# Fused top-k attention, mixture of experts and cosine layer: w_out converted beside the first experts, expert weights loaded ahead, six candidate segments

## The chip, the cores and the metric

One core of a Trainium2 chip runs the whole program. The metric is device time in microseconds of one launch, from host arrays in the chip's memory to the finished output there; lower is better. Engines are named as in the profile: PE is TensorE (matmul), DVE is VectorE, ACT is ScalarE, POOL is GpSimd, and SP is SyncE, which issues nearly all DMA transfers from one queue, in order.

## The reference, cut to what matters

Three layers follow one another: attention that keeps the 32 largest scores of each row, a mixture of experts with a skip test, and a dense layer pair with a cosine gate.

```python
# attention: q, k, v are [4, 8, 576, 64]
scores = scale * np.matmul(q, k.transpose(0, 1, 3, 2))
kth = np.partition(scores, -32, axis=-1)[..., -32:-31]
scores = np.where(scores >= kth, scores, -1e9)
attn = exp(scores - max); attn /= attn.sum(-1, keepdims=True) + 1e-9
x = (attn @ v) as [2304, 512]

# experts: w_gate [512, 8], w1 [8, 512, 1024], w2 [8, 1024, 512]
do_compute = x @ w_skip > 0
e_idx = argmax(x @ w_gate); gate_w = its softmax probability
y = gate_w * (relu(x @ w1[e_idx]) @ w2[e_idx])
x = x + y where do_compute, else x

# dense pair: w_in [512, 2048], w_out [2048, 512], stored as float64
h = x @ w_in
out = (h * cos(h)) @ w_out
```

[...]

## The kernel before, in words

**Two groups.** The 2304 tokens are two groups of 1152 (two batches each). For a group, `attend(n)` (line 559) runs 72 times: 8 heads times 9 tiles of 128 rows. One such call is named a step here; n counts from 0 to 71 for group 0 and from 72 to 143 for group 1. After its attention a group is stored, routed to experts (`route`, line 743), sent through the experts (`experts`, line 850) and through the dense pair (`cosine`, line 988). Group 0's experts and cosine layer run on PE between the attention steps of group 1; group 1's experts and cosine layer come last.

**A step.** PE computes scores into one of three PSUM slots `s` (L587). DVE takes the 8 largest of each of `NSEG` = 8 segments of 72 columns (L596), giving 64 candidates, and finds the 24th largest of these by three maxima (L606) and two replacements (L608). ACT computes the exponentials (L613) and, from the 24th candidate, which scores lie above it and how many (L617, L620). PE shifts those out of the way (L625), DVE finds the 8 largest of the rest (L633, 584 wide) and so the 32nd of the row, and masks (L636). ACT and POOL split the weights into two float16 parts (L639, L643, L644), SP transposes them by DMA (L647), and PE weighs the values (L654 to L663). A row is right as long as the count of scores at or above the 24th candidate is below 32; the flags from L1106 on test this for all rows, and a general path outside the plan repeats what fails.

**Converting the float64 weights.** `load_f64` (line 424 on) does one slice of 65,536 numbers (512 KB) at a time: SP loads it into one of two stage buffers `wbuf[0:2]` (L431), ACT takes the sign (L436), DVE shifts and merges the two integer halves (L437, L439), POOL and ACT build a range check (L441, L446), ACT scales (L443), POOL sets the sign (L448), ACT writes the high float16 part (L450) and POOL the low one (L451). The scratch is a ring of two for the bits and one buffer each for sign and magnitude; it lies in the gate slots 4 to 7 of the cosine layer (`r_gT`). There are 16 slices of w_in (`load_win`) and 16 of w_out (`load_wout`). In the kernel before, w_out has a buffer of its own, and its slices are declared after step 38 (`EARLY`) with priorities n + 4 + 2i, which is 42 to 72: among the steps of group 0.

**The expert weights.** Each expert has 4 tiles of w1 and 4 of w2, 512 KB each, 64 tiles in all per group, loaded by L862. Group 0's experts use them in float32 straight from the four buffers `wbuf[2:]` (the ring `r_wall`), so tile k waits until tile k - 4 has been read by PE. The first four may start when step 38 has passed its normalisation (`gate[n0 - 34]`). PE's work on them is at L911 (first matrix) and L942 (second).

**What sets the order.** All work is declared as units with an engine, a cost, what they read and write, and a priority (`Plan.add`). `Plan.run` (line 156) simulates the engines with these costs and issues the instructions in the order in which the simulation starts them; on each engine the ready unit with the smallest priority goes first, and that order is then fixed on the chip. Units with a priority from 900 up belong to group 0's experts and cosine layer; for ACT and DVE 1000 is taken off, and for POOL 2000, so there they go ahead of most attention steps, while on PE and SP they come after:

```python
SOONER = {"ACT": 1000.0, "DVE": 1000.0, "POOL": 2000.0}
if prio >= 900:
    prio -= self.SOONER.get(eng, 0.0)
```

SP issues no further load while the planned DMA backlog is over 3.5 us.

Of the kernel before, what the change touches and what calls it, by code (L numbers as in the profile page):

```python
# [10 lines left out]
F32 = mybir.dt.float32  # L11
F16 = mybir.dt.float16
# [191 lines left out]
def kernel(  # L204
# [14 lines left out]
    nc = tc.nc  # L219
    B, H, S, D = q.shape  # L220
    NT, DM = out.shape
# [9 lines left out]
    NFF = FF // P  # L231
# [4 lines left out]
    ESC = 1.0 / (math.sqrt(D) * SQ * SQ)  # L236
    HUGE = 2.0 ** 40 / ESC
    N = NG * H * NJ
    NSEG = 8
    EARLY = 38  # L240

    dram = ctx.enter_context(tc.tile_pool(name="dram", bufs=1, space=DRAM))
    x_d = [dram.tile([GT, DM], F32, name=f"x_d{g}") for g in range(NG)]
# [14 lines left out]
    def sb(name, shape, dt=F32):  # L258
        return pool.tile([P] + list(shape), dt, name=name)
# [4 lines left out]
    def as16(ap, *shape):  # L264

        t = ap.bitcast(F16)
        return view(t, *shape)
# [92 lines left out]


    win = Slot(sb("win16", [KD, 2, FF], F16), NFF)
    wout = Slot(sb("wout16", [NFF, 2, DM], F16), NFF)
    SPACE = 136064
    arena = Arena(sb("arena", [SPACE // 4]), SPACE)

    def ring(n, shape, dt=F32, parts=1):
        return Ring([arena.new(shape, dt, parts) for _ in range(n)])

    r_qkv = ring(2, [10, D])  # L370
    r_h16 = ring(2, [9, 2, D], F16, 2)
# [8 lines left out]
    for sl in r_v.slots:  # L380
        sl.ap = (view(sl.ap, 10, D + 1), view(sl.ap[:, 10 * (D + 1):], 10, D))
        nc.vector.memset(sl.ap[0][:, :, D:D + 1], SV)
    r_cand = ring(3, [8 * NSEG], F32, NSEG)
    r_m = ring(4, [48], F32, 5)
# [1 line left out]
    mj = ring(2, [P])  # L386
    xs = arena.new([NJ, DM], F32, 3)
    wbuf = [arena.new([1024]) for i in range(6)]
    free = [arena.at(4096 * i, [1024], F32) for i in range(9)]
    r_stage = [Ring(wbuf[:2]), Ring(wbuf[:2] + free[:5])]  # L390
    r_split = [Ring(wbuf[2:]), Ring(wbuf[2:] + free[5:])]
    r_wall = Ring(wbuf[2:])
    r_sq = ring(1, [DM], F16)
    x0 = xs.lo

    def after(base, n, shape, dt=F32, parts=1):

        size = 2048
        return Ring([arena.at(base + size * i, shape, dt, parts) for i in range(n)])

    r_x16 = [ring(2, [2, DM], F16, 2), after(36864, 2, [2, DM], F16, 2)]
    r_xT = [ring(2, [DM]), after(36864 + 4096, 2, [DM])]
    r_xg = [ring(3, [DM]), after(x0, 3, [DM])]
    r_gT = [ring(8, [DM], F32, 2), after(x0 + 6144, 4, [DM], F32, 2)]
    r_ob = [ring(2, [DM]), after(x0 + 14336, 2, [DM])]
# [9 lines left out]
    def dve(n):  # L415
        return (n + 64) / 960.0
# [57 lines left out]
                wmx[:, i:i + 1], pw.ap, axis=AX.X, op=OP.max), r=[pw], w=[mxs], prio=prio)  # L474

    def load_wout(i, prio):
        load_f64(wout, wout[i], wout.ap[:, i:i + 1, 0, :], wout.ap[:, i:i + 1, 1, :],
                 w_out.rearrange("(c p) d -> p c d", p=P)[:, i:i + 1, :], SO, NFF + i, prio)


    n0 = H * NJ
    heads = {}
    gate = Slot(parts=N)
# [75 lines left out]
    def attend(n):  # L559
# [33 lines left out]
        p, r, jk = r_p.new(), r_r.new(), r_jk.new()  # L593
        sw = S // NSEG
        for i in range(NSEG):
            add("DVE", dve(sw), lambda i=i: nc.vector.max(cand.ap[:, 8 * i:8 * i + 8], S_[:, sw * i:sw * i + sw]),  # L596
# [253 lines left out]
    def experts(g, prio):  # L850
        gs, gidx, sidx, rs = routed[g]
        wide = WIDE[g]
        scat = []
        xg, xT, hT, w = {}, {}, {}, {}

        def weight(e, s, i):
            if s == 0:
                src = w1[e].rearrange("(c p) f -> p c f", p=P)[:, :, i * 256:(i + 1) * 256]
            else:
                src = w2[e].rearrange("(c p) d -> p c d", p=P)[:, 2 * i:2 * i + 2, :]  # L860
            st = (r_wall if wide else r_stage[g]).new()
            add("SP", 0.5, lambda: nc.sync.dma_start(st.ap.rearrange("p (a b) -> p a b", a=src.shape[1]), src),  # L862
                r=[gate[n0 - 34]] if g == 0 else [], w=[st], prio=prio[0] - 5, lat=0.6, dma=1.5)
            if wide:
                w[e, s, i] = (st, view(st.ap, KD, 256) if s == 0 else view(st.ap, 2, DM))
                return
            sp = r_split[g].new()
            wv = as16(sp.ap, 2, 1024)
            sc = S2 if s else S1
            add("ACT", act(1024), lambda: nc.scalar.activation(wv[:, 0, :], st.ap, AF.Copy, scale=sc),  # L870
                r=[st], w=[sp], prio=prio[0] - 4)
            add("DVE", dve(1024), lambda: nc.vector.scalar_tensor_tensor(
                wv[:, 1, :], st.ap, sc, wv[:, 0, :], op0=OP.mult, op1=OP.subtract),
                r=[st], w=[sp], prio=prio[0] - 4)
            w[e, s, i] = (sp, as16(sp.ap, 2, KD, 256) if s == 0 else as16(sp.ap, 2, 2, DM))
# [112 lines left out]
    def cosine(g, prio):  # L988
# [45 lines left out]
        def output(i, fc, po):  # L1034
            gt, gv = gts[i, fc // 4]

            def mm():
                for n_, (sg, sw) in enumerate(((0, 0), (1, 0), (0, 1))):
                    nc.tensor.matmul(po.ap, gv[:, sg, fc % 4, :], wout.ap[:, fc, sw, :],  # L1039
                                     start=(fc == 0 and n_ == 0), stop=(fc == NFF - 1 and n_ == 2))  # L1040

            add("PE", 0.66, mm, r=[gt, wout[fc]], w=[po], prio=prio[0])
            prio[0] += 1
# [11 lines left out]
        for i in range(NJ + 1):  # L1055
            if i + 1 < NJ:
                turn(i + 1)
            po = ring_m[1 + 2 * g].new(True) if i else None
# [17 lines left out]
        load_win(i, 4.0 * i + 10.0)  # L1076
    for n in range(n0):
        attend(n)
        if n == EARLY:
            for i in range(NFF):  # L1080
                load_wout(i, n + 4.0 + 2.0 * i)
    recut(third_ps, [s2], half, "half", "right")
    store_x(0, n0 + 0.0)
    route(0, n0 - 10.0)
# [2 lines left out]
    recut(wide_ps, s_slots, quarter, "quarter", "left")  # L1087
    prio = [1000.0]
    experts(0, prio)
    cosine(0, prio)  # L1090
    store_x(1, 0.0)
    route(1, 0.0)
# [2 lines left out]
    prio = [4000.0]  # L1095
# [353 lines left out]
```

## Time and profile before

| | |
|---|---|
| median of 3 runs | 1208.11 us (1207.56 to 1214.32) |
| the profiled execution's own time | 1203.05 us |
| its span, first to last instruction | 1200.8 us |
| busy PE, DVE, ACT, POOL | 968.3, 878.0, 803.6, 576.5 us |
| share of the span | 81%, 73%, 67%, 48% |
| mean granted TensorE clock | 0.907 of full speed |
| DMA moved | 191.44 MB, mean 159 GB/s |

All rows further down are from that one execution. A busy time is the time in which the engine had an instruction in it; durations of single instructions overlap where an engine is pipelined. [...] "DMA" is the mean busy share of the 16 DMA engines. "L596" is line 596 of the kernel.

### The profile page before, as it was taken

What the parts mean: (1) busy time and instruction counts of PE and PEld (TensorE: products, weight loads), DVE (VectorE), ACT (ScalarE), POOL (GpSimd) and SP (SyncE); (2) the same over time, 40 slices, a digit from 0 to 9 for tenths busy, and PEclk for the clock granted to TensorE, in tenths of its full rate; (3) what the DMA queues carried; (4) which work ended last, traced back from release to release, by engine and by line L of the source; (5) the groups of instructions that cost most, each with busy time, mean ns of one, the idle gap of its engine ahead of it and who ended that gap; (6) DMA issues with size and microseconds to landing.
All of it is one profiled execution on the core that took longest, in us unless ns stands there. A gap on an engine that the chain in (4) does not pass through costs nothing. (4 is left out here: it accounts for less than half of the span.)

```text
span 1200.8 us, 27693 instructions
## 1 busy us (share of the span) xinstructions
PE 968.3 (81%) x9891; PEld 689.2 (57%) x9892; DVE 878.0 (73%) x3187; ACT 803.6 (67%) x1657; POOL 576.5 (48%) x591
## 2 busy tenths in 40 slices
PE   2656666665667788889868999998998999999996
PEld 1334444333445566666637766776775756777773
DVE  6999999998897876767787888996577874322221
ACT  5888898888776555656668777875466657543441
POOL 5989999888553434444443534342123321222121
PEclk9999996555657699999978999999999999999999
DMA  8767868778669599999997465449479972210100
GB/s 190 162 155 173 158 150 184 191 165 174 136 144 198 108 264 228 248 274 274 269 212 132 87 98 129 103 125 265 79 174 313 333 224 73 61 37 19 36 10 22
DMA packets 343124, 191.44 MB, mean 159 GB/s; under 512 B 260546, under 2 KB 313794, under 8 KB 342976
## 3 DMA queue, kind: packets, MB, share of 16 engines
q1 hardware_dynamic: 340416, 183.30, 65.7%
q0 software_dynamic: 2560, 6.28, 1.7%
q8 instruction: 79, 1.29, 0.5%
q14 instruction: 69, 0.57, 0.2%
HBM read 107.50 MB, written 18.35 MB: 105 GB/s over the span
## 5 line engine op out<-in xcount | busy, mean ns | idle before, releaser
L1009 PEld LDWEIGHTS <-win 128*128 128x128 f16 x3456 | 216.5, 99 | 49.8 <-issue 1.7
L596 DVE MAX8 arena<-s 128x8 f32<-128x72 f32 x1152 | 197.0, 224 | 26.7 <-PE s L587 26.3
L1031 POOL TENSOR_TENSOR arena<-arena 128x512 f16<-128x512 f32 x72 | 84.8, 1178 | 237.9 <-ACT arena L1030 207.0
L587 PE MATMUL s<-arena 128*128 128x320 f16 (+7 forms) x800 | 130.9, 330 | 56.5 <-DVE arena L636 37.6
L644 POOL TENSOR_TENSOR arena<-arena 128x512 f16<-128x512 f32 x144 | 170.3, 1183 | 0.0
L654 PE MATMUL o_bank<-arena 128*128 128x65 f16 (+1 forms) x640 | 99.2, 221 | 76.4 <-DMA arena<-arena 72.5
L636 DVE SCALAR_TENSOR_TENSOR arena<-s,kth,arena 128x576 f32<-128x576 f32 x144 | 116.5, 809 | 48.4 <-PE s L625 41.8
L1009 PE MATMUL half<-arena,win 128*128 128x128 f16 x2112 | 147.9, 222 | 0.0
L587 PEld LDWEIGHTS <-arena 128*128 128x128 f16 (+1 forms) x800 | 86.5, 123 | 106.2 <-issue 57.1
L1026 DVE SCALAR_TENSOR_TENSOR arena<-arena 128x512 f32<-128x512 f32 x72 | 51.6, 717 | 124.4 <-ACT arena L1023 124.4
L639 ACT ACTIVATE arena<-arena 128x576 f16<-128x576 f32 x144 | 97.7, 678 | 63.8 <-DVE arena L636 50.7
L654 PEld LDWEIGHTS <-arena 128*128 128x128 f16 (+1 forms) x640 | 71.9, 117 | 118.4 <-DMA arena<-arena 107.8
L643 POOL TENSOR_TENSOR arena<-arena 128x64 f16<-128x64 f32 x144 | 50.7, 352 | 184.4 <-ACT arena L639 169.5
L1039 PE MATMUL m_bank<-wout,arena 128*128 128x512 f16 x480 | 126.8, 381 | 1.1 <-ACT arena L1048 0.9
L613 ACT ACTIVATE arena<-s,arena 128x576 f32<-128x576 f32 x144 | 105.3, 732 | 12.9 <-POOL arena L644 9.9
L625 PE MATMUL s<-arena,plus 128*128 128x320 bf16 (+1 forms) x288 | 76.7, 359 | 44.1 <-DVE kth L633 40.4
L633 DVE MAX8 kth<-s 128x8 f32<-128x584 f32 x144 | 110.1, 765 | 1.2
L617 ACT ACTIVATE arena<-s,arena 128x576 bf16<-128x576 f32 x144 | 105.8, 735 | 2.3
L1039 PEld LDWEIGHTS <-arena 128*128 128x128 f16 x864 | 75.2, 98 | 48.5 <-issue 1.7
L606 DVE MAX8 arena<-arena 128x8 f32<-128x64 f32 x432 | 94.5, 219 | 6.3
L620 ACT ACTIVATE arena<-arena 128x576 bf16<-128x576 bf16 x144 | 97.4, 677 | 1.2
L656 PE MATMUL o_bank<-arena 128*128 128x64 f16 (+1 forms) x640 | 98.0, 218 | 0.0
(189 smaller groups left out, 2324.8 us busy)
## 6 DMA issues: line engine op xcount, KB each, us to landing
arena<-in_moe_w_dram SPq DMA_DIRECT2D x128, 512.0 KB
arena<-in_moe_w_in_dram SPq DMA_DIRECT2D x16, 512.0 KB
arena<-in_moe_w_out_dram SPq DMA_DIRECT2D x16, 512.0 KB
x_d<-arena SPq DMA_DIRECT2D x8, 768.0 KB
arena<-arena SPq DMA_DIRECT2D x32, 144.0 KB
arena<-x_d SPq DMA_DIRECT2D x18, 256.0 KB
out_dram<-arena SPq DMA_DIRECT2D x18, 256.0 KB
arena<-in_q_dram SPq DMA_DIRECT2D x16, 256.0 KB
```

Of the source, the lines that this page charges most:

```text
L587: nc.tensor.matmul(S_[rows, o:o + n_], qT.ap[:, i, cols], kT.ap[:, kc:kc + n_], start=(i == 0 and o < 512), stop=(i == 1), skip_group_chec ...
L596: add("DVE", dve(sw), lambda i=i: nc.vector.max(cand.ap[:, 8 * i:8 * i + 8], S_[:, sw * i:sw * i + sw]), r=[s], w=[cand[i]], prio=pr - 0.5)
L613: lambda: nc.scalar.activation(p.ap, S_, AF.Exp, bias=M[:, 40:41], scale=ESC),
L617: lambda: nc.scalar.activation(r.ap, S_, AF.Relu, bias=M[:, 41:42], scale=ESC),
L633: add("DVE", 0.68, lambda: nc.vector.max(kth[g][:, z:z + 8], s.ap), r=[s], w=[found[n], in_turn], prio=pr)
L636: add("DVE", 0.73, lambda: nc.vector.scalar_tensor_tensor(p.ap, S_, kth[g][:, z + 7:z + 8], p.ap, op0=OP.is_ge, op1=OP.mult), r=[s, found[ ...
L639: add("ACT", act(S), lambda: nc.scalar.activation(pc.ap[:, 0:S], p.ap, AF.Copy), r=[p], w=[pc[0]], prio=pr + 0.5)
L644: nc.gpsimd.tensor_tensor(pc.ap[:, S + ST:], p.ap[:, 0:SM], pc.ap[:, 0:SM], op=OP.subtract)
L654: nc.tensor.matmul(oj[rows, 0:D + 1], pT.ap[:, c, rows], vh[:, 5 * b + c, :], start=(c == 0), stop=False)
L656: nc.tensor.matmul(oj[rows, 0:D], pT.ap[:, c, rows], vl[:, 5 * b + c, :], start=False, stop=False)
L1009: nc.tensor.matmul(view(ph.ap, 4, P)[:, f, :], win.ap[:, c, sw, f0:f0 + P], xv[:, sx, c, :], start=(n == 0), stop=(n == 3 * KD - 1))
L1039: nc.tensor.matmul(po.ap, gv[:, sg, fc % 4, :], wout.ap[:, fc, sw, :], start=(fc == 0 and n_ == 0), stop=(fc == NFF - 1 and n_ == 2))
```

## The change

Three edits go together. The candidates of a step come from six segments of 96 columns and no more from eight of 72 (48 candidates in place of 64). The memory of the converted w_out becomes part of the arena, and its first use there is as eight more buffers (`ahead`) for expert tiles: the first twelve tiles of group 0's experts (eight in `ahead`, four in `wbuf[2:]`) may be loaded once step 38 has passed, and the thirteenth and later ones go through the four buffers as before. And the 16 slices of w_out are declared after the experts of group 0, with priorities 1050 + 5i, where the experts' run from 1000 to 1128; slice pair 2k, 2k + 1 lies in the memory of expert tile k.

```diff
-    NSEG = 8
-    EARLY = 38
+    NSEG = 6
...
-    wout = Slot(sb("wout16", [NFF, 2, DM], F16), NFF)
-    SPACE = 136064
+    SPACE = 168832
     arena = Arena(sb("arena", [SPACE // 4]), SPACE)
...
+    ahead = [arena.at(4096 * i, [1024], F32) for i in range(NFF // 2)]
+    wout = [arena.new([2, DM], F16) for _ in range(NFF)]
+    base0 = arena.top
...
-    free = [arena.at(4096 * i, [1024], F32) for i in range(9)]
+    free = [arena.at(base0 + 4096 * i, [1024], F32) for i in range(9)]
...
     r_wall = Ring(wbuf[2:])
+    first_w = list(ahead + wbuf[2:])
+    r_wall.k = 0
...
-            st = (r_wall if wide else r_stage[g]).new()
+            early = wide and bool(first_w)
+            st = first_w.pop(0) if early else (r_wall if wide else r_stage[g]).new()
             add("SP", 0.5, lambda: nc.sync.dma_start(st.ap.rearrange("p (a b) -> p a b", a=src.shape[1]), src),
-                r=[gate[n0 - 34]] if g == 0 else [], w=[st], prio=prio[0] - 5, lat=0.6, dma=1.5)
+                r=[gate[n0 - 34]] if early else [], w=[st], prio=prio[0] - 5, lat=0.6, dma=1.5)
...
-                    nc.tensor.matmul(po.ap, gv[:, sg, fc % 4, :], wout.ap[:, fc, sw, :],
+                    nc.tensor.matmul(po.ap, gv[:, sg, fc % 4, :], wout[fc].ap[:, sw, :],
...
     for n in range(n0):
         attend(n)
-        if n == EARLY:
-            for i in range(NFF):
-                load_wout(i, n + 4.0 + 2.0 * i)
...
     experts(0, prio)
+    for i in range(NFF):
+        load_wout(i, 1050.0 + 5.0 * i)
     cosine(0, prio)
```

## Rows read from the trace of the kernel before

**Rows 1.** Busy time by stage: PE, PEld, DVE, ACT, POOL, then PEclk, DMA, GB/s.
```profile
core 0: us, PE busy (x) PEld busy (x) DVE busy (x) ACT busy (x) POOL busy (x), PEclk, DMA share, GB/s
30.00:155.00 125.00, 79.27 (x617) 50.62 (x615) 121.85 (x512) 107.96 (x252) 114.49 (x112) 1.00 0.76 164
155.00:300.00 145.00, 90.35 (x739) 58.62 (x740) 136.66 (x586) 126.68 (x297) 131.25 (x126) 0.64 0.76 171
300.00:360.00 60.00, 39.75 (x332) 25.72 (x331) 53.96 (x258) 44.51 (x105) 33.12 (x39) 0.60 0.65 139
360.00:413.00 53.00, 36.68 (x391) 29.32 (x391) 43.60 (x182) 30.60 (x66) 21.67 (x25) 0.65 0.73 155
413.00:613.00 200.00, 173.77 (x1475) 125.65 (x1475) 143.65 (x620) 121.25 (x261) 83.69 (x97) 0.99 1.05 254
613.00:643.00 30.00, 21.59 (x262) 17.60 (x261) 24.84 (x106) 23.76 (x59) 11.65 (x14) 0.72 0.76 167
643.00:813.00 170.00, 160.54 (x2030) 121.26 (x2027) 147.33 (x588) 133.89 (x290) 75.60 (x85) 0.99 0.55 113
...
878.00:988.00 110.00, 100.67 (x1095) 70.75 (x1093) 88.72 (x92) 72.92 (x87) 28.04 (x16) 1.00 0.97 277
988.00:1200.00 212.00, 200.40 (x2208) 143.22 (x2205) 62.42 (x107) 93.41 (x160) 41.80 (x37) 0.99 0.15 37
```

**Rows 2.** Groups of DVE by line, 155 to 300 us: count, busy us, mean ns.
```profile
L596 DVE MAX8 arena<-s 128x8 f32<-128x72 f32 x232 | 40.9, 223 | 0.5 <-PE s L587 0.2
...
L633 DVE MAX8 kth<-s 128x8 f32<-128x584 f32 x30 | 22.8, 760 | 0.0
...
L439 DVE SCALAR_TENSOR_TENSOR arena<-arena 128x512 int32<-128x512 int32 x16 | 15.7, 980 | 0.0
L437 DVE TENSOR_SCALAR arena<-arena 128x512 int32<-128x512 int32 x15 | 12.7, 846 | 3.9 <-DMA arena<-in_moe_w_out_dram 3.9
```

**Rows 3.** The candidate maxima (L596) alone, by stretch: busy us and count.
```profile
300.00:360.00 60.00, 19.33 (x108) 0.60 0.65 139
```

**Rows 4.** Waits of DVE from 300 to 360 us.
```profile
DVE s L631 <- PE s L625: 3.0, 3, 1.6
```

**Rows 5.** Line L431 on SP, loads of w_out: ns min/median/max, first and last start.
```profile
L431 SPq DMA_DIRECT2D arena<-in_moe_w_out_dram x16: 333/512/579, 147.7 to 282.2; - x16
```

**Rows 6.** Timeline of DVE around 330 us: start, us, count.
```profile
330.19 1.07 DVE L596 MAX8 arena<-s 128x8 f32<-128x72 f32 x7
```

**Rows 7.** Waits of SP's queue, 30 to 155 us: us in total, times, longest.
```profile
SPq L431 <- POOL arena L441: 4.4, 6, 1.0
```

**Rows 8.** Waits of PE and of SP's queue, 413 to 613 us.
```profile
PE o_bank L654 <- DMA arena<-arena: 21.2, 17, 2.9
...
SPq L862 <- PE s L625: 24.9, 19, 4.0
```

**Rows 9.** Groups of ACT by line, whole span: the four of a conversion.
```profile
L446 ACT ACTIVATE arena<-arena,wlim 128x512 f32<-128x512 f32 x32 | 22.7, 710 | 2.5 <-POOL arena L441 2.4
...
L436 ACT ACTIVATE arena<-arena 128x512 f32<-128x512 f32 x32 | 20.9, 653 | 1.0 <-DMA arena<-in_moe_w_in_dram 1.0
L443 ACT ACTIVATE arena<-arena 128x512 f32<-128x512 f32 x32 | 19.9, 621 | 4.5 <-DVE arena L439 4.4
...
L450 ACT ACTIVATE wout<-arena 128x512 f16<-128x512 f32 x16 | 9.9, 617 | 0.6 <-POOL arena L448 0.6
```

**Rows 10.** Lines L437 and L439: ns min/median/max, first and last start.
```profile
L437 DVE TENSOR_SCALAR arena<-arena x32: 402/922/1575, 9.6 to 286.0; 128x512 int32<-128x512 int32 x32
...
L439 DVE SCALAR_TENSOR_TENSOR arena<-arena x32: 665/694/1709, 10.0 to 289.3; 128x512 int32<-128x512 int32 x32
```

**Rows 11.** First starts of expert, hidden and output matmuls, same columns.
```profile
L911 PE MATMUL half<-arena x320: 272/275/422, 413.5 to 587.0; 128*128 128x128 f32 x160
...
L1009 PE MATMUL half<-arena,win x2112: 216/219/314, 631.1 to 1163.5; 128*128 128x128 f16 x192
...
L1039 PE MATMUL m_bank<-wout,arena x480: 376/379/634, 649.5 to 1116.6; 128*128 128x512 f16 x160
```

More of the change, by code (lines that the diff above doesn't have):

```diff
@@ L399, in after @@
         return Ring([arena.at(base + size * i, shape, dt, parts) for i in range(n)])
-    r_x16 = [ring(2, [2, DM], F16, 2), after(36864, 2, [2, DM], F16, 2)]
-    r_xT = [ring(2, [DM]), after(36864 + 4096, 2, [DM])]
+    r_x16 = [ring(2, [2, DM], F16, 2), after(base0 + 36864, 2, [2, DM], F16, 2)]
+    r_xT = [ring(2, [DM]), after(base0 + 36864 + 4096, 2, [DM])]
     r_xg = [ring(3, [DM]), after(x0, 3, [DM])]
@@ L476, in load_wout @@
     def load_wout(i, prio):
-        load_f64(wout, wout[i], wout.ap[:, i:i + 1, 0, :], wout.ap[:, i:i + 1, 1, :],
+        load_f64(wout[i], wout[i], wout[i].ap[:, 0:1, :], wout[i].ap[:, 1:2, :],
                  w_out.rearrange("(c p) d -> p c d", p=P)[:, i:i + 1, :], SO, NFF + i, prio)
```

## The prediction, made before the changed kernel was run

> **What bounds the kernel now.** I read the stages first, the busy time of each engine in ten stretches of the span [rows 1]. Three regimes show. From 30 to 300 us, the attention of group 0 with the weight conversions beside it, VectorE (DVE) is busy 121.85 of 125 us and 136.66 of 145 us, and TensorE (PE) only 63%. From 300 to 360 us, when the conversions are over, DVE has dropped to 53.96 of 60. From 413 us on PE is the fullest engine: 173.77 of 200 us beside the first experts, 160.54 of 170 beside the cosine layer, 92% in the second experts and 95% in the last 212 us. Between them lie two thin places, 360 to 413 (routing of group 0) and 613 to 643 (from experts to cosine), where no engine is full.
>
> Second, the instruction groups of DVE between 155 and 300 us [rows 2]: 232 candidate maxima (L596), 8 to a step, so 29 attention steps in 145 us, 5.0 us a step. The two DVE operations of a conversion take 0.98 us (L439) and 0.85 us (L437) there. Third, the same candidate line between 300 and 360 us: 108 maxima, 13.5 steps, 4.44 us a step [rows 3]. That is the pace without conversions. What DVE waits for there is mostly PE (L625, 3.0 us) [rows 4]: the chain of one step begins to show once DVE has room.
>
> So a microsecond taken from DVE before 360 us ends the first stage earlier by up to a microsecond; one added to DVE, ACT or POOL after 413 us costs only if PE comes to wait for it.
>
> **The change part by part.** All terms are set against the profiled execution, 1203.05 us; the median of the runs shown, 1208.11, lies 5 us above it, and that is added at the end.
>
> *Where the conversions go.* Sixteen loads of w_out (L431) were issued from 147.7 to 282.2 us [rows 5]: all in the DVE-bound stage. In the changed kernel they are declared after the first experts with late priorities, but a priority only orders what is ready. A load needs just a stage buffer (of two), so the first two conversions will still run in group 0 up to the float16 write (L450). That write needs the memory that expert tile 0 holds until PE has read it, so the third stops at the two-buffer ring of bits, and four loads are through. Fourteen pairs of DVE operations move. At 0.98 + 0.85 = 1.83 us a pair [rows 2] that is 26 us of DVE; by the pace it is 0.56 us a step over 29 steps, 16 us for sixteen, so 14 us for fourteen [rows 2, 3]. The bounds are 14 and 26; I take 19, since the freed stretch will look like 300 to 360 us, where DVE is 90% busy and not 95%.
>
> *Six segments.* Seven candidate maxima back to back take 1.07 us, the last 0.22 of them alone, so one follows the other in 0.14 us [rows 6]. The 584-wide maximum takes 760 ns, the 72-wide 223 [rows 2]: 537 ns for 512 elements, 1.05 ns each. A 96-wide one then takes 0.165 us in line. Eight at 0.14 are 1.12 us, six at 0.165 are 0.99: 0.13 us less a step. The five operations on the candidates (three L606, two L608) go from 64 to 48 elements, 17 ns each, 0.085 us. Together 0.215 us, over 72 steps 15.5 us. Where DVE has 10% idle, half may be lost in waits: 30 steps at full and 42 at half value give 11 us. I take 15.
>
> [...]
>
> *First stage in sum:* 19 + 15 = 34 us, between 25 (14 + 11) and 41. The w_in conversions stay; POOL is 92% busy beside them [rows 1], and is next in line if DVE gets faster there, which is why I do not take the upper end.
>
> *Weights ahead.* Instead of 4 expert tiles 12 are loaded behind the same gate (step 38), 8 more issues on SP and 4.2 MB; 12 of 16 w_out loads leave that stage, 6.3 MB. An issue holds SP for some 0.51 us (as L431 [rows 5]), so 8 more cost 4 us of SP and 12 fewer give 6 back; DMA is 0.76 busy there [rows 1]. I count 0, with 4 us either way; the cover is DVE's own work, and if it is gone, what stands behind is the transposes (L647) that PE's weighing waits for.
>
> *Beside the first experts.* This stage gets 12 loads more and 8 fewer: 2.1 MB at its 254 GB/s [rows 1], 8 us of a DMA that is already at 1.05. Each w_out load waits on SP for its stage buffer, as in the first stage: 4.4 us for 6 waits [rows 7], 0.73 each, 9 us for 12, with transposes and expert loads queued behind. The 8 tiles ahead need no release: SP waits 24.9 us in 19 times there for PE to free a tile [rows 8], 1.3 each, so 10 us go. The conversions' ACT and DVE work is given precedence over the steps of attention. DVE has 56 us idle in 200, ACT 79 [rows 1], against 14 times 1.83 = 26 us, and 14 times 2.60 (0.65 + 0.62 + 0.71 + 0.62) [rows 9] = 36 us: it fits in, if the order written beforehand holds. New on ACT is the wait of L450 for PE's read of an expert tile; queued behind it are the exponentials of the steps (L613), for which PE waits. Planned after that read, it costs nothing by itself; the slip below is its price. The order counts 0.94 us for the DVE pair; at their fastest the pair takes 0.40 + 0.67 = 1.07 us [rows 10], so 0.13 us of slip times 14 is 2 us, and at 1.83 us it is 12; I take 3, nearer the fast end, because POOL is 42% busy there and not 90%. Sum 8 + 9 - 10 + 3 = 10 us given back. Bounds: -10 (only the freed waits count) and +62 (all ACT and DVE time of the 14 lies in the path of attention, and PE waits).
>
> The operation L437 takes 0.40 us at its fastest, 0.92 in the middle and 1.58 at most [rows 10], beside a POOL 90% busy. [...]
>
> *Are they in time?* At the pace of before, (282.2 - 147.7) / 15 = 9.0 us each [rows 5], 14 conversions last 126 us, from about the first expert tile on. The hidden layer of group 0 starts 218 us after the experts do (631.1 against 413.5), and w_out is first read at 649.5 [rows 11]. The cosine layer's gate slots 4 to 7 share memory with the conversion's scratch, and are wanted at its second tile, later still. No cost; if the loads came only with their late priorities, the last would end some 9 us after the last expert load, still ahead of 649.5.
>
> *Later stages.* Six segments take 7.7 us more from DVE between 643 and 813 us (36 steps), but PE is 94% busy there, and its work is unchanged: I count 0, with 0 and 7 as bounds. PE's granted clock, 0.64 from 155 to 300 us after 1.00 with the same 63% of PE busy, gives no term; PE is not the bound there.
>
> Sum: 1203.05 - 34 + 10 = 1179, as a median 1184 us.
>
> **Rivals.**
> 1. *Deeper gain* (41 us in the first stage, nothing given back, 5 us of DVE later): 1203 - 46 + 5 = 1162 us. For it: DVE and ACT have room beside the experts [rows 1]. Against: SP's waits [rows 7, 8] and a DMA at 1.05.
> 2. *Gain lost on the way.* The first stage ends 25 to 34 us earlier, and PE waits as much more beside the experts, because its instructions stand in a fixed order and its commonest wait there is for the transposes (L654, 21.2 us [rows 8]), which stand behind the w_out loads on SP. 1208 us, within 12. Against: these loads are 12 among more than 60.
> 3. *Slower: the conversions stand in front of the attention of group 1.* Their ACT and DVE work has precedence, and a step needs both engines in turn; if none of it falls into idle time, the stage grows by 14 times (2.60 + 1.83) = 62 us, and 62 - 34 is 28 us more: 1236 us. It turns slower from the point where over half of that work is in the path. For it: DVE waits for PE, PE for transposes, so idle time there is not free time. Against: idle DVE of 56 us and ACT of 79.
> 4. *The fallback fires.* With six segments of eight candidates the threshold row check (L1106) can fail. From the reference's inputs with seed 0, no row of 18,432 fails with eight segments or six; the largest count rises from 28 to 31, and 31 is the last that passes. A firing would read all weights again, 50 MB at 254 GB/s, some 200 us: over 1400 us.
>
> **How the numbers follow.** Forecast 1184 us (1170 to 1198) with 56%, deeper gain 16%, lost on the way 14%, slower 11%, fallback 3%. About 1%, 12 us, is what a measurement of this kernel can tell from no change. Below 1196 lie rival 1, nearly all of the forecast and a little of rival 2: 0.70. Within 1%: the rest of the forecast and most of rival 2, 0.15. Slower: rivals 3 and 4 and the edge of 2, 0.15. The range of 1154 to 1213 leaves out the slower cases and the deepest end.
>
> **What would show it.** Right: the first expert matmul (L911, now at 413.5 us [rows 11]) near 380; steps before it at about 4.3 us with two-operation conversions only until about 160 us; two pairs of L437 and L439 for w_out in group 0 and fourteen beside the experts; experts to cosine some 210 us long instead of 200. Six 96-wide maxima with a spacing near 0.165 us. Wrong: a first stage that ends later than 390 us (then another engine or the chain bounds it); PE waits for transposes beside the experts well over 35 us (rival 2 or 3); an L1039 that waits for w_out or for a gate slot; any launch of the general path.

## The result and the profile after

The changed kernel takes 1193.28 us (median of 4 runs, 1189.03 to 1195.44) against 1207.84 for the kernel before beside it. The ratio is 0.9896, with a 95% interval of 0.9859 to 0.9933: 1.0% faster, a gain of 14.6 us between the medians where 24 were forecast (1184). The profiled execution took 1189.03 us, with a span of 1187.3 in place of 1200.8. In the changed kernel's file the lines stand 5 to 6 further down: L596 is L601 there, L911 is L917, L1009 is L1015.

The busy time by stage, in the same columns as [rows 1] (PEclk is the granted clock of TensorE as a share of full speed). The first two stretches are those of before, the third lies where the stage of the first experts now begins and ends:

```profile
30.00:155.00 125.00, 75.46 (x627) 48.85 (x627) 114.86 (x457) 109.43 (x253) 112.75 (x111) 0.62 0.76 156
155.00:300.00 145.00, 91.87 (x818) 61.32 (x817) 126.88 (x558) 109.76 (x253) 82.00 (x95) 0.64 0.76 167
402.00:608.00 206.00, 176.14 (x1448) 128.82 (x1448) 161.42 (x578) 146.41 (x323) 135.49 (x137) 0.97 1.00 255
```

Read it against [rows 1]. DVE has fallen from 121.85 to 114.86 of 125 us and from 136.66 to 126.88 of 145: the work did leave it. Beside the experts ACT went from 121.25 of 200 us to 146.41 of 206 and POOL from 83.69 to 135.49: the conversions arrived there. But the first stage did not end 34 us earlier. The first expert matmul, which started at 413.5 us [rows 11], now shows at 402.7, and the hidden layer at 627.2 after 631.1:

```profile
L917 PE MATMUL half<-arena x320: 272/275/421, 402.7 to 578.4; 128*128 128x128 f32 x160
...
L1015 PE MATMUL half<-arena,win x2112: 216/219/311, 627.2 to 1149.9; 128*128 128x128 f16 x192
```

So 10.8 us were won in the first stage, 5.8 were given back beside the experts (205.4 us from their first to their last matmul, after 199.6), and the later stages are shorter by the rest, 8.5 of the 13.5 us of span. From the first expert matmul to the end of the span it is 2.7 us less in all (784.6 us after 787.3).

The attention of group 0 by itself ended 16.6 us earlier. Its last step shows in the 72nd of the 584-wide maxima, here before and then in the changed kernel:

```profile
368.10 0.75 DVE L633 MAX8 kth<-s 128x8 f32<-128x584 f32 x1
```

```profile
351.49 0.77 DVE L638 MAX8 kth<-s 128x8 f32<-128x584 f32 x1
```

From there to the first expert matmul lies the routing of group 0. It took 51.2 us in place of 45.4, and seven steps of group 1 began in it in place of six. So only 10.8 of the 16.6 us reach the first expert matmul.

Where the conversions went, first on SP (loads of w_out up to 400 us), then the groups of DVE between 395 and 620 us:

```profile
L436 SPq DMA_DIRECT2D arena<-in_moe_w_out_dram x4: 335/429/519, 152.8 to 172.9; - x4
```

```profile
L442 DVE TENSOR_SCALAR arena<-arena 128x512 int32<-128x512 int32 x14 | 17.5, 1248 | 0.1
L444 DVE SCALAR_TENSOR_TENSOR arena<-arena 128x512 int32<-128x512 int32 x14 | 15.1, 1080 | 0.1
```

Four loads went ahead in group 0, and 14 of the 16 DVE pairs ran beside the experts. A pair costs more there than it did, on average: 1.25 + 1.08 = 2.33 us after 1.83 [rows 2]. Two of the L442 make up most of their 17.5 us, with 5.20 and 4.29 us; the other twelve take 0.67 us on average.

The waits of PE beside the experts, 402 to 608 us, have changed their kind (us in total, times, longest). Those for the transposes, 21.2 us before [rows 8], are down to 2.0; PE now waits for DVE instead:

```profile
PE s L630 <- DVE kth L638: 12.5, 11, 3.6
...
PE o_bank L659 <- DMA arena<-arena: 2.0, 3, 0.9
```

### The profile page after: what moved, and what is told of

It is laid out like the page before. It is cut to its first block, busy times and chain, and to the rows that moved or that the text cites. A ratio compares the mean times of both kernels' runs of the same rounds, so it can differ in the third digit from the quotient of the medians.

```text
span 1187.3 us, 27421 instructions
## 1 busy us (share of the span) xinstructions
PE 953.9 (80%) x9891; PEld 681.9 (57%) x9892; DVE 864.5 (73%) x2899; ACT 804.5 (68%) x1657; POOL 567.9 (48%) x591
## 4 chain that ended last, share of the span: by engine, by line
PE 31%; DMA 21%; DVE 19%; issue 11%; POOL 9%; ACT 5%; SPq 2%; POOLq 0%; DVEq 0%; ACTq 0%
DMA arena<-arena 12%; PE half L1015 4%; PE quarter L1015 4%; PE quarter L1045 4%; DVE arena L601 4%; DMA arena<-in_moe_w_dram 3%; PE m_bank L1045 3%; POOL arena L649 3%; DVE arena L641 3%; PE half L1045 3%; DVE kth L638 2%; PE s L630 2%; DMA arena<-x_d,gidx 2%; PE s L592 2%; DMA arena<-in_v_dram 2%
## 5 line engine op out<-in xcount | busy, mean ns | idle before, releaser
L1015 PEld LDWEIGHTS <-win 128*128 128x128 f16 x3456 | 213.9, 98 | 48.8 <-issue 3.0
L601 DVE MAX8 arena<-s 128x8 f32<-128x96 f32 x864 | 176.3, 249 | 32.6 <-PE s L592 32.0
L592 PE MATMUL s<-arena 128*128 128x320 f16 (+7 forms) x800 | 126.9, 322 | 53.2 <-DVE arena L641 34.0
L1032 DVE SCALAR_TENSOR_TENSOR arena<-arena 128x512 f32<-128x512 f32 x72 | 54.0, 750 | 128.5 <-ACT arena L1029 128.5
L1015 PE MATMUL half<-arena,win 128*128 128x128 f16 x2112 | 145.0, 221 | 1.9 <-DMA arena<-arena 1.1
L592 PEld LDWEIGHTS <-arena 128*128 128x128 f16 (+1 forms) x800 | 84.7, 120 | 95.1 <-issue 48.9
L659 PEld LDWEIGHTS <-arena 128*128 128x128 f16 (+1 forms) x640 | 70.6, 114 | 97.2 <-DMA arena<-arena 83.6
L1045 PE MATMUL m_bank<-arena 128*128 128x512 f16 x480 | 124.9, 379 | 0.7 <-ACT arena L1054 0.7
L630 PE MATMUL s<-arena,plus 128*128 128x320 bf16 (+1 forms) x288 | 73.8, 347 | 46.8 <-DVE kth L638 42.3
L630 PE MATMUL s<-arena,minus 128*128 128x320 bf16 (+1 forms) x288 | 73.0, 343 | 37.0 <-ACT arena L618 24.3
L625 ACT ACTIVATE arena<-arena 128x576 bf16<-128x576 bf16 x144 | 97.6, 678 | 1.0
L661 PE MATMUL o_bank<-arena 128*128 128x64 f16 (+1 forms) x640 | 95.9, 214 | 0.0
```

Of the source, the lines that this page charges most:

```text
L592: nc.tensor.matmul(S_[rows, o:o + n_], qT.ap[:, i, cols], kT.ap[:, kc:kc + n_], start=(i == 0 and o < 512), stop=(i == 1), skip_group_chec ...
L630: nc.tensor.matmul(S_[:, o:o + n_], by, r.ap[:, o:o + n_], start=False, stop=True, skip_group_check=True)
L659: nc.tensor.matmul(oj[rows, 0:D + 1], pT.ap[:, c, rows], vh[:, 5 * b + c, :], start=(c == 0), stop=False)
L1015: nc.tensor.matmul(view(ph.ap, 4, P)[:, f, :], win.ap[:, c, sw, f0:f0 + P], xv[:, sx, c, :], start=(n == 0), stop=(n == 3 * KD - 1))
L1045: nc.tensor.matmul(po.ap, gv[:, sg, fc % 4, :], wout[fc].ap[:, sw, :], start=(fc == 0 and n_ == 0), stop=(fc == NFF - 1 and n_ == 2))
```

## The experiments

Each kernel was timed against the kernel before on its own chip, so the ratios are what can be compared. In the table, "pace" is us a step, worked out as length of the stretch over the mean number of steps that three DVE lines show in it (candidate maxima over segments, the 584-wide maximum, the masking). It goes by whole instructions: one 584-wide maximum more or less between 30 and 155 us moves it by 0.06. 30 to 155 us has the w_in conversions beside it in all kernels; 200 to 300 us has the w_out conversions beside it only where they were not moved. "Experts" is the time from the first to the last float32 expert matmul.

| kernel | ratio to before (95%) | pace 30-155 | pace 200-300 | first expert matmul | experts |
|---|---|---|---|---|---|
| before | 1 | 4.87 | 5.00 | 413.5 | 199.6 |
| changed | 0.9896 (0.9859-0.9933) | 4.80 | 4.41 | 402.7 | 205.4 |
| 1: six segments alone | 1.0000 (0.9977-1.0023) | 4.80 | 4.95 | 419.1 | 202.6 |
| 2: moved, eight segments | 0.9961 (0.9937-0.9985) | 4.93 | 4.46 | 399.6 | 211.5 |
| 3: no loads ahead | 0.9916 (0.9886-0.9946) | 4.87 | 4.23 | 393.1 | 210.3 |
| 4: no conversion of w_out | 0.9747 (0.9694-0.9801) | 4.80 | 4.35 | 398.9 | 192.4 |
| 5: one POOL operation less | 1.0007 (0.9978-1.0036) | 4.88 | 4.43 | 402.6 | 209.8 |
| 6: conversions behind the steps | 1.0018 (0.9989-1.0046) | 4.87 | 4.43 | 405.8 | 211.9 |
| 7: conversions spread | 0.9951 (0.9921-0.9981) | 4.80 | 4.41 | 405.4 | 213.3 |
| 8: two score slots | one run, 1269.3 us to 1203.1 | 5.92 | 5.36 | 462.4 | 213.5 |
| 9: changed, second order | 0.9981 (0.9953-1.0008) | 4.88 | 4.66 | 410.3 | 207.2 |
| 10: before, second order | 1.0021 (0.9996-1.0046) | 4.93 | 4.90 | 415.9 | 198.9 |
| 11: measured costs in the plan | 1.0083 (1.0053-1.0113) | 4.92 | 4.69 | 418.6 | 184.9 |
| 12: changed, third order | 1.0003 (0.9975-1.0032) | 4.93 | 4.41 | 403.9 | 209.0 |

**1 and 2: each half of the change alone.** On the kernel before:

```diff
-    NSEG = 8
+    NSEG = 6
```

> The kernel before with six segments and nothing else. Theory A: in group 0 the pace of the steps is not set by DVE but by POOL beside the w_in conversions and by the chain of a step after them, so the 0.2 us less DVE work a step brings nothing there: first expert matmul between 409 and 414 us (413.5 before), total 0 to 6 us below before. Theory B (the prediction's term): DVE is the bound and six segments take 11 to 15 us from group 0: first expert matmul near 400 us, total 11 to 18 us below before.

and on the changed kernel:

```diff
-    NSEG = 6
+    NSEG = 8
```

> The changed kernel with eight segments again, so only the moved conversions and the loads ahead are left. Theory A: nearly the whole gain of group 0 stays, first expert matmul at 403 to 406 us (402.7 in the changed kernel), total 0 to 6 us above the changed kernel. Theory B: 11 to 15 us of it go, first expert matmul at 414 to 418 us, total near 1206 us, no better than before.

Six segments alone gained nothing (1203.24 us against 1203.44), and the first expert matmul came at 419.1 us, later than either theory expected and later than before. The 31st of the 584-wide maxima starts at 172.9 us in kernel 1 and in the kernel before alike. The first expert matmuls of kernel 1:

```profile
L911 PE MATMUL half<-arena x320: 272/275/426, 419.1 to 591.1; 128*128 128x128 f32 x160
```

The move with eight segments kept the whole gain of the first stage:

```profile
L917 PE MATMUL half<-arena x320: 272/275/422, 399.6 to 573.5; 128*128 128x128 f32 x160
```

Its total is 5.1 us below before. So theory A held for group 0. Against the changed kernel the total is 8 us higher by the ratios, just outside theory A's 0 to 6; the two intervals nearly meet (0.9859 to 0.9933, 0.9937 to 0.9985), and kernels 9 and 12 below show that an order alone makes as much. The busy times of DVE go with it. With eight segments and the conversions moved (kernel 2, columns as in rows 1)

```profile
30.00:155.00 125.00, 77.55 (x622) 49.02 (x620) 121.29 (x510) 107.86 (x252) 114.48 (x112) 0.65 0.75 164
```

and with six segments and no conversion moved (kernel 1)

```profile
30.00:155.00 125.00, 75.18 (x628) 48.64 (x628) 115.90 (x457) 109.49 (x253) 113.11 (x111) 0.65 0.76 157
```

DVE is busy 121 us in the one and 116 in the other from 30 to 155 us, and the pace is 4.93 and 4.80; over all kernels it is 4.87 to 4.93 with eight segments and 4.80 to 4.93 with six (three slots). DVE's busy share of 97% in [rows 1] was no sign that a shorter DVE would shorten the step. What changes the pace is whether conversions stand beside the steps: 4.9 to 5.0 us with those of w_out, 4.2 to 4.7 without.

**3: no loads ahead.**

```diff
-    first_w = list(ahead + wbuf[2:])
+    first_w = list(wbuf[2:])
...
-    def load_f64(dst, part, hi, lo, src, scale, i, prio):
+    def load_f64(dst, part, hi, lo, src, scale, i, prio, after=()):
...
-            w=[st], prio=prio, lat=0.6, dma=1.5)
+            r=list(after), w=[st], prio=prio, lat=0.6, dma=1.5)
...
-                 w_out.rearrange("(c p) d -> p c d", p=P)[:, i:i + 1, :], SO, NFF + i, prio)
+                 w_out.rearrange("(c p) d -> p c d", p=P)[:, i:i + 1, :], SO, NFF + i, prio, [gate[n0 - 1]])
```

> The changed kernel in which only four expert tiles are loaded early, as before, the eight further buffers stay unused, and each w_out load waits for the last step of group 0. Theory A (the loads ahead only make room and cost group 0 little): first expert matmul at 400 to 403 us, and the stretch from there to the end of the first experts some 5 to 12 us longer than the changed kernel's 205 us, because all sixteen slices and all tiles now load there; total 3 to 10 us above the changed kernel. Theory C (the twelve loads in a row at 217 to 248 us took away what the prediction had counted for group 0): first expert matmul at 385 to 393 us, total 5 us or more below the changed kernel.

The first expert matmul came at 393.1 us, the stretch of the experts took 210.3, and the total, 0.9916, cannot be told from the changed kernel's. This is between the two theories: the loads ahead seem to cost group 0 (pace 4.23 without them, against 4.35 in kernel 4, which keeps them and has no conversion either, and 4.41 in the changed kernel) about 6 us to the first expert matmul (398.9 - 393.1), and to give 5 us back beside the experts (210.3 - 205.4). Each of the two numbers compares single orders, and kernels 9 and 12 move them by up to 7.6 and 3.6 us without any change of work. In the changed kernel they are issued in a row:

```profile
L868 SPq DMA_DIRECT2D arena<-in_moe_w_dram x12: 458/578/975, 216.6 to 247.9; - x12
```

In sum the loads ahead are worth nothing that can be told from no change.

**4: the price of the conversions at their new place.**

```diff
     for i in range(NFF):
-        load_wout(i, 1050.0 + 5.0 * i)
+        add("POOL", 0.6, lambda i=i: nc.gpsimd.memset(wout[i].ap, 0.0), w=[wout[i]], prio=1050.0 + 5.0 * i)
```

> The changed kernel without the conversions of w_out: in their place POOL clears the memory of w_out, 16 short fills. This leaves out the loading and conversion of w_out (the output is zero), so that their price at the new place shows. If it is the predicted 10 us: the stretch of the first experts is 195 us in place of 205, and the total 7 to 12 us below the changed kernel. If they are hidden there: 0 to 3 us below. If they hold up the attention of group 1 in earnest (the slower rival's mechanism, only hidden by the gain): 20 us or more below.

1171.42 us, ratio 0.9747, which is 0.0149 below the changed kernel's or 18 us of 1204. Twice the 10 us forecast, short of the slower rival's 62. In the stretch of the experts (beside it the third row of the changed kernel above, 402 to 608 us: DVE 161.42 of 206, POOL 135.49)

```profile
399.00:591.00 192.00, 172.71 (x1460) 125.06 (x1460) 134.17 (x546) 117.63 (x255) 97.32 (x113) 0.99 1.00 241
```

the same PE work, with 32 attention steps begun beside it in both, takes 192.4 us and not 205.4: 13 us of the price lie there, 3.8 before the first expert matmul (398.9 after 402.7), and little more than 1 behind. Against the kernel before it is 0.0253 or 30 us. If the other two edits are worth nothing, as kernels 1 and 3 say, the conversions cost some 30 us at the old place and 18 at the new one, and the move saved 12. The 18 and the 12 hang on the changed kernel's own order: against the mean of its three orders below (0.996) they are some 26 and 5 us.

**5: is POOL the bound beside the w_in conversions?**

```diff
-        add("POOL", gp(512), lambda: nc.gpsimd.tensor_tensor(mag.ap, fl, sgn.ap, op=OP.mult),
-            r=[st, sgn], w=[mag], prio=prio)
...
-            lambda: nc.scalar.activation(mag.ap, mag.ap, AF.Relu, bias=wlim, accum_out=wchk[:, i:i + 1]),
-            w=[mag, chk[i]], prio=prio)
+            lambda: nc.scalar.activation(mag.ap, fl, AF.Relu, bias=wlim, accum_out=wchk[:, i:i + 1]),
+            r=[st], w=[mag, chk[i]], prio=prio)
```

> The changed kernel with one POOL operation less in each of the 32 conversions (1.34 us): the range check no longer multiplies by the sign first, so it leaves negative numbers unchecked. DVE's work stays. Theory A (POOL bounds the steps beside the w_in conversions): pace from 30 to 155 us 4.5 us a step or less (4.8 in the changed kernel, and 4.8 to 4.93 in all kernels so far), first expert matmul at or before 397 us (402.7), total 8 to 20 us below the changed kernel. Rival (the chain of a conversion or of a step bounds it, no single engine): pace within 0.1 of 4.8, total 0 to 6 us below.

```profile
30.00:155.00 125.00, 78.14 (x622) 49.59 (x621) 113.76 (x458) 108.86 (x254) 98.01 (x101) 0.67 0.81 167
```

POOL is busy 98 of 125 us in place of 113, and the pace is 4.88. POOL is not the bound either; theory A's name for it fell. The total did not fall below the changed kernel but came out at 1.0007, with the hidden layer at 627.8 us (627.2) and the attention of group 1 ending 18 us later (833.0 against 815.3): less work, another order, a slower program.

**6 and 7: other precedence for the conversions.** Kernel 6:

```diff
-        load_wout(i, 1050.0 + 5.0 * i)
+        load_wout(i, 880.0 + 0.5 * i)
```

Kernel 7:

```diff
-        load_wout(i, 1050.0 + 5.0 * i)
+        load_wout(i, n0 + 6.0 + 3.0 * i)
```

> The changed kernel with the priorities of the w_out slices at 880 + 0.5 i in place of 1050 + 5 i, so that they lose the precedence on ACT, DVE and POOL and go behind all attention steps that are ready. Theory D (the 19 us that the conversions cost in group 1 come from their precedence over the attention, rival 3's mechanism): stretch of the first experts 193 to 199 us in place of 205, total 6 to 15 us below the changed kernel. Theory E (they come from the engines' time itself, in whatever order): stretch 202 to 208, total within 4 us. If they then come too late, PE waits at L1045 for w_out and the total rises.

> The changed kernel with the w_out slices at priorities 78 + 3 i, that is spread among the steps of group 1 from step 78 to 123, neither ahead of all nor behind all. Theory D: between the changed kernel and the one with the conversions behind the steps, total 2 to 10 us below the changed kernel. Theory E: within 4 us of the changed kernel.

The stretch of the experts grew to 211.9 and 213.3 us, and the totals are 1.0018 and 0.9951, about 15 and 7 us above the changed kernel by the ratios. The longer stretch is not waiting of PE, since 35 attention steps begin in it, in place of 32. PE's idle time is the better measure there. In kernel 6 (405.8 to 618.3 us, columns as in rows 1)

```profile
405.80:618.30 212.50, 182.74 (x1529) 130.56 (x1528) 170.72 (x619) 155.47 (x347) 146.75 (x147) 0.98 1.03 260
```

it is 29.8 us, in kernel 7 30.7 us, and in the changed kernel 29.9 of 206 us. Theory D finds no support: with precedence taken away PE stands idle as long. The edits change more than precedence, though. With priorities below 1000 the w_out loads also go ahead of expert loads on SP, and the fourteen conversions ran closer together (L442 from 411 to 549 and from 411 to 538 us; in the changed kernel from 408 to 607). Theory E expected totals within 4 us of the changed kernel's, and both are further off, on the slow side; kernels 9 and 12 below show that an order alone can do that much, so the loss is not evidence for either place.

**8: how much is the chain of a step?**

```diff
-    ring_s = [Ring(s_slots + [s2]), Ring(s_slots)]
+    ring_s = [Ring(s_slots), Ring(s_slots)]
```

> The changed kernel with two PSUM score slots instead of three for group 0. Theory F (the pace in group 0 is the time for which a step holds its score slot, divided by the number of slots): 4.4 us with three slots means a slot is held for 13.2 us, and two slots give up to 6.6 us a step, at least 5.3 because less queues in front of it; first expert matmul at 470 us or later (402.7), total 60 us or more above. Rival (an engine's own time is the bound, DVE at 86% or POOL): pace at most 4.8 after the w_in conversions, first expert matmul before 430 us.

```profile
200.00:330.00 130.00, 77.00 (x623) 48.69 (x622) 96.27 (x413) 82.71 (x179) 51.70 (x63) 0.53 0.65 143
```

Pace 5.36 where no conversion runs and 5.92 beside those of w_in, first expert matmul at 462.4 us, total 66 us above before. The pace is above the 5.3 expected, the first expert matmul some 8 us short of the 470. The rival is out for two slots: with two steps in flight every engine is emptier (DVE 74%) and the step is slower. A slot is held for 2 times 5.36 = 10.7 us with two slots, and 3 times 4.41 = 13.2 with three, so the holding time is not fixed. One reading is a step's chain of some 10 us, lengthened by what queues in front of each of its links. That the chain bounds the pace at three slots too is argued from this and from kernels 1 and 5; a fourth slot, which would test it, was not tried.

**9, 10 and 12: what the order alone is worth.** One planned cost of the conversion is changed by 0.02 us; the work stays the same. Kernel 9 is the changed kernel with this edit, kernel 10 the kernel before with it:

```diff
-        add("DVE", 0.34, lambda: nc.vector.tensor_scalar(ti, words[:, :, 1], 3, None, op0=OP.logical_shift_left),
+        add("DVE", 0.36, lambda: nc.vector.tensor_scalar(ti, words[:, :, 1], 3, None, op0=OP.logical_shift_left),
```

and kernel 12 is the changed kernel with

```diff
-        add("DVE", 0.34, lambda: nc.vector.tensor_scalar(ti, words[:, :, 1], 3, None, op0=OP.logical_shift_left),
+        add("DVE", 0.32, lambda: nc.vector.tensor_scalar(ti, words[:, :, 1], 3, None, op0=OP.logical_shift_left),
```

> The changed kernel with one planned cost altered by 0.02 us (L442: 0.36 for 0.34). No work is added or taken away; only the order written beforehand may fall out a little differently. If the gain belongs to the change itself: ratio to before within 0.004 of the changed kernel's 0.990. If it hangs on the order that happened to come out: off by 0.006 or more.

> The kernel before with the same planned cost altered by 0.02 us (L437: 0.36 for 0.34). Same work. If the order hardly matters: within 0.4% of before. Otherwise off by 0.6% or more, either way.

> The changed kernel with the same planned cost altered the other way (L442: 0.32 for 0.34). Same work, a third order. If 0.990 was the change's own worth and 0.998 a bad draw: ratio to before 0.987 to 0.993. If the order decides within a band of about 1%: anywhere from 0.985 to 1.0, first expert matmul between 399 and 412 us, earlier than the 413 to 416 us of the two orders of the kernel before.

The same change gives 0.9896, 0.9981 and 1.0003 in three orders; the kernel before gives 1 and 1.0021 in two. The first expert matmul of the two further orders of the changed kernel starts at 410.3 and 403.9 us. A difference of up to 1.1% hangs on how ties and near ties fall in the plan. The mean of the changed kernel's three is 0.996, that of the two before 1.001: by these the edits themselves are worth some 0.5%, and the rest of the 1.0% measured is the order that came out. Three orders that differ by 1.1% leave the 0.5% uncertain. The eight kernels with the move and three slots (changed, 2, 3, 5, 6, 7, 9, 12) say much the same: their mean ratio is 0.997, that of the three without it (before, 1, 10) 1.001, and the changed kernel is the lowest of the eight. Part of its 1.0% may also lie in the 1207.84 us beside it, since the kernel before took 1202.5 to 1204.7 us beside the others.

**11: measured costs in the plan.** The planned costs of the conversion's DVE and POOL operations as below; likewise its second POOL product at 1.38, and its ACT operations at 0.64 (0.9 for the one with the sum).

```diff
-        add("DVE", 0.34, lambda: nc.vector.tensor_scalar(ti, words[:, :, 1], 3, None, op0=OP.logical_shift_left),
+        add("DVE", 0.85, lambda: nc.vector.tensor_scalar(ti, words[:, :, 1], 3, None, op0=OP.logical_shift_left),
...
-        add("DVE", 0.6, lambda: nc.vector.scalar_tensor_tensor(ti, words[:, :, 0], 29, ti, op0=OP.logical_shift_right,
+        add("DVE", 1.0, lambda: nc.vector.scalar_tensor_tensor(ti, words[:, :, 0], 29, ti, op0=OP.logical_shift_right,
...
-        add("POOL", gp(512), lambda: nc.gpsimd.tensor_tensor(mag.ap, fl, sgn.ap, op=OP.mult),
+        add("POOL", 1.34, lambda: nc.gpsimd.tensor_tensor(mag.ap, fl, sgn.ap, op=OP.mult),
```

> The changed kernel with the measured durations of a conversion put into the plan: 0.85 and 1.0 us for the two on DVE (0.34 and 0.6), 0.64 and 0.9 on ACT (0.52 to 0.70), 1.34 and 1.38 on POOL (1.11). Same work in another order. Theory G (part of the 19 us that the conversions cost in group 1 is slip, the planned order not fitting the chip): stretch of the first experts at or below 201 us, total 4 to 10 us below the changed kernel. Theory E (it is the engines' and the step's own time): within 4 us of it.

The experts took 184.9 us, 20 less than in the changed kernel, as theory G wanted and more. Only 28 attention steps begin in this stretch, in place of 32, which is 8.5 us less work for PE; its idle time there is 17.9 us, 12 less than in the changed kernel (29.9):

```profile
418.60:604.10 185.50, 167.59 (x1366) 120.49 (x1366) 139.90 (x507) 130.55 (x290) 126.85 (x127) 0.99 1.03 273
```

But the first expert matmul came at 418.6 us, and the attention of group 1 ended 20 us later than in the changed kernel (835.8 against 815.3). Total 1.0083. Of the 20.9 us that its span is longer than the changed kernel's, 15.9 lie before the first expert matmul. A truer cost for one kind of unit moved the waiting to other stages.

No kernel here that does the whole work is faster than the changed one; kernel 3 is its equal.

## Why the prediction was right or wrong

The side and the range were right: faster by over 1% had the largest chance, and 1193.28 lies within 1154 to 1213. The size is short: two terms of the sum were too large, the six segments (15, measured 0) and the conversions taken from group 0 (19, measured 10.8). One of the prediction's own signs of being wrong came true: the first stage ended at 402.7 us, later than 390, "then another engine or the chain bounds it". And that the gain came out over 1% is in part luck, since the same change in two other orders took 0.998 and 1.000 of the time before.

*Where the conversions go: right to the unit.* Two converted in group 0, four loads through, fourteen DVE pairs beside the experts, the write L450 (now L455) waiting for PE: it starts at 405.3 us, 2.6 us after the first expert matmul. *In time* was right too, with less room than thought: the first operation (L442) of the 14 starts from 408.0 to 607.3 us, 15.3 us apart and not 9.0, and the first use of w_out is at 647.3 us, with no wait for it.

*Six segments: duration right, value wrong.* Five 96-wide maxima back to back took 0.90 us, a lone one 0.25 (timeline of DVE around 270 us, changed kernel):

```profile
270.81 0.90 DVE L601 MAX8 arena<-s 128x8 f32<-128x96 f32 x5
```

That is (0.90 - 0.25) / 4 = 0.163 us, forecast 0.165. But the 15 us that this should have given in the first stage are 0 there: the pace beside w_in is 4.87 to 4.93 with eight segments and 4.80 to 4.93 with six, and kernel 1 gained nothing. The step that failed is the sentence that a microsecond taken from DVE before 360 us ends the first stage earlier by up to a microsecond, and with it the lower bound of 11: an engine busy 97% was taken for the bound. [rows 4] pointed the other way: as soon as DVE had room, from 300 to 360 us, it waited for PE (L625, 3.0 us).

*The conversions' 19 us* were 10.8 in the changed kernel. Over the eight whole kernels with the move, three slots and the old planned costs or near them (changed, 2, 3, 5, 6, 7, 9, 12) the first expert matmul starts at 402.9 us on average, over the three without it (before, 1, 10) at 416.2: 13 us, just under the bound of 14, the value that came from the pace. The bound from the pace was the better reading than the one from DVE's durations (26). By the last 584-wide maximum of group 0 it is 17.4 us (352.4 after 369.8 on average); the routing behind it takes 50.5 us with the move and 46.4 without. Why it is longer was not tested; the prediction had the routing unchanged.

*Beside the experts* the forecast gave back 10 us. The same kernels average 209.8 us with the move and 200.4 without, 9.4 us (8.5 without kernels 6 and 7, in which three more steps run there); the changed kernel itself, at 5.8, drew a good order. So the sum is near, but its terms are not: PE's waits for transposes, on which rival 2 stood, fell from 21.2 to 2.0 us, and the slip of the DVE pair, taken as 3 us, would be 14 times 2.33 - 0.94, which is 19 us, by the prediction's own working. And the price against no conversion at all was 18 us over the whole program. The 3 us placed the pair near its fast end because POOL was 42% busy there, and no run shows a price that goes by POOL's busy share. What the runs show in its place: the conversions brought their own POOL work with them, 135 of 206 us, and at this share of 66% the pair took 2.33 us, more than the 1.83 at 90%. For single operations, in both kernels, the five with no POOL instruction beside them took 0.42 to 0.43 us (L437, now L442) and the other five 0.67 to 0.69 us (L439, now L444). Every longer one had POOL work beside it, but 25 of the 59 L439 and L444 that had it took no more than 0.70 us either. The longest L442

```profile
444.65 5.20 DVE L442 TENSOR_SCALAR arena<-arena 128x512 int32<-128x512 int32 x1
```

lies beside five POOL instructions without a pause (444.57 to 449.57 us), and PE waited 3.2 us for the 584-wide maximum behind it. That POOL held it up is read from this coincidence; no kernel tested it by itself.

*Weights ahead* were counted 0, and kernel 3, which does without them, takes the same time within its interval.

*Later stages* were counted 0, and the changed kernel won 8.5 us there. The other two orders of it show from the last expert matmul to the end of the span 581.0 and 591.4 us, the changed kernel 579.2, before 587.7: this part is order, not a term.

*The rivals.* Rival 1, the deeper gain (1162 us), did not happen. Rival 2, the gain lost on the way, is what kernels 9 and 12 show (0.998 and 1.000), by another mechanism than its transposes: the order. Rival 3 did not happen; kernels 6 and 7 give no sign that its mechanism, the precedence, is what costs. Rival 4 did not happen. What the forecast lacked altogether is a rival in which the fixed order falls out differently, worth about 1% either way.

What stays open: which link of the step's chain the conversions lengthen. DVE's and POOL's share were each lowered without effect beside the w_in conversions; ACT, busy 105 to 109 of 125 us from 30 to 155 us in all these kernels with three slots, was not.

## What to carry to other kernels

A busy share of 97% does not show that an engine is the bound: here DVE lost 6 of its 121 us and the steps came no faster (4.80 to 4.93 us a step with six segments, 4.87 to 4.93 with eight), while one buffer less made them slower (5.36 us a step from 200 to 300 us in place of 4.41). Compare the pace of the same step with and without the other work beside it, in the trace at hand, and take that difference as the gain. The length of a stage is comparable between kernels only if the same work runs in it: count the steps, or compare the idle time of the engine that is full there. And where a planner fixes the order, change a cost by a hair and time it again before a per cent is put down to an edit.

## What the runs showed of the hardware that was not expected

The granted TensorE clock of the profile did not tell how fast matmuls ran in the first 180 us of the kernel before. In its profiled execution it reads 1.00 from 60 to 150 us and falls between 180 and 200 us (0.90, then 0.50), after some 150 us with PE busy about 64%. In the changed kernel it falls between 40 and 60 us, after PE had been busy 5.8 of 10 us (30 to 40 us), and is 0.59 from 60 to 150 us:

```profile
40.00:50.00 10.00, 5.31 (x47) 3.25 (x46) 8.68 (x42) 9.01 (x23) 8.19 (x9) 0.71 0.73 133
50.00:60.00 10.00, 5.90 (x45) 3.81 (x44) 9.78 (x35) 7.57 (x18) 9.77 (x10) 0.50 0.85 172
```

This is no effect of the change: kernel 10, the kernel before with 0.02 us in its plan, reads 0.66 from 30 to 155 us and kernel 1 0.65, and 22 other executions of the kernel before have a mean of 0.839 to 0.881 over the whole span, where the profiled one has 0.907.

And the matmuls of this stage are the same at 1.00 in the one kernel and at 0.59 in the other. Those that weigh the values follow one another with 64 or 65 columns each. In the kernel before, at a granted 1.00, they start 0.05 us apart:

```profile
100.65 0.24 PE L658 MATMUL o_bank<-arena 128*64 128x65 f16 x1
100.70 0.25 PE L654 MATMUL o_bank<-arena 128*64 128x65 f16 x1
```

In the changed kernel, where PE is full, they start 0.03 us apart, at a granted 1.00 too:

```profile
702.65 0.19 PE L663 MATMUL o_bank<-arena 128*128 128x65 f16 x1
702.68 0.19 PE L659 MATMUL o_bank<-arena 128*128 128x65 f16 x1
```

The median distance of these is 54 to 55 ns from 60 to 150 us in both kernels, at 1.00 and at 0.59, and 29 to 33 ns from 640 to 790 us. Inside the changed kernel's early stage the distance goes with the reading: 54 ns from 68.1 to 105.5 us, at a granted 0.50, and 29 ns from 64.7 to 67.9 us, at 1.00; a single one (L661) takes 243 ns in the first and 192 in the second. In the kernel before it is 54 ns too from 188 to 256 us, at 0.50. Read by these, PE ran mostly as it does at a reading of 0.50 in the early stage of both kernels, and the 1.00 of [rows 1] for 30 to 155 us is not borne out by its matmuls. Why the profile reads 1.00 there is open. The 320-column score matmuls agree: 449 ns before and 437 ns after from 60 to 150 us, and 299 ns in the changed kernel from 640 to 790 us.
